# Adding the last three token tiles of expert 0 from PSUM instead of from memory, and routing tiles 5 to 8 one step sooner

## The chip, the cores and the metric

The kernel runs on one core of a Trainium2 chip, as one program. The metric is device time in microseconds (us) of one execution. Within the core TensorE (PE) multiplies, VectorE (DVE), ScalarE (ACT) and GpSimd (POOL) do the rest of the arithmetic, and SyncE (SP) issues most transfers; each engine works through its own queue in order and waits for the others by semaphores.

## The reference, cut to what matters

```python
x = attention(q, k, v, proj)                       # 1536 tokens x 512
h = x @ w_in; e = exp(h - max(h)); solu = h * e / (sum(e) + 1e-9)
x = (layernorm(solu) * g_ln) @ w_out               # 1536 x 512, hidden 1024
logits = x @ w_gate                                # 8 experts
e_idx = argmax(logits); gate_w = softmax(logits)[e_idx]
eom = 1 / (1 + exp(-(x @ w_output_gate)))
for e in range(8):
    m = e_idx == e
    out[m] = gate_w[m] * eom[m, e] * (relu(x[m] @ w1[e]) @ w2[e])
```

## The kernel before, in words

The program has three stages on PE: attention (to about 210 us), the dense block (class Ffn) on twelve tiles of 128 tokens (to about 370 us), and the eight experts (class Experts) to the end. Products are made of float32 split into a high and a low part (hi, lo), three products for one.

In the dense block each tile i goes through `up` (two halves of 512), `solu` (DVE and ACT), `turn` (PE transposes), `down` (24 products into `y` or `h`, copied by ACT to `row`), `flip` (PE transposes of the row), and `logits` or `batch` (products with the gate weights). Tiles are routed in GROUPS: 0 to 4, 5 to 8, 9 and 10, and 11. `route(g)` returns two lists: `first` finds the expert of each token (DVE), and `rest` counts, by small PE products (`ranks`), which place the token has among those of its expert, works out a `slot`, and then POOL writes (`scatter`) the 515-column rows (512 values, gate, token number, expert) to those slots of a buffer in memory, `scratch`, by one indirect transfer for each tile. Each expert has CAP = 256 slots. Lists of `route` wait in `stages` until `flush` runs them, or until they are merged with `solu`; PE, DVE, ACT and POOL each run their share in the order in which the program was written.

In the stage of the experts `rows(e)` reads the 256 rows of an expert back from `scratch` (two transfers on SP), `turn(e)` transposes them on PE and splits them into `xh` and `xl` (ACT and DVE), `up(e)` and `down(e)` make the two layers, and `finish` scales and writes to the output. `fetch(u)` loads a unit of weights (1 MB) and `splitw(u)` makes its high and low part, mostly an expert ahead. `early` splits units 0 and 1 during the end of the dense block.

The two stages meet so: the rows of expert 0 are read when all twelve scatters have landed (`rows`, line 1033, with a wait for each scatter), and until they come PE does 28 products that nobody reads (`warm`, line 1068). SP's queue holds, in this order, the reads of experts 0, 1 and 2 (six transfers) and then the loads of the weight units from 4 on.

Of the kernel before, what the change touches and what calls it, by code (L numbers as in the profile page):

```python
# [8 lines left out]
F32 = mybir.dt.float32  # L9
F32R = mybir.dt.float32r  # L10
# [562 lines left out]

def merge(a, b):
    k = -(-len(b) // max(1, len(a)))
    for f in a:
        f()
        for g in b[:k]:
            g()
        b = b[k:]  # L580
    for g in b:
        g()


class Ffn:
# [3 lines left out]
    def __init__(self, tc, ctx, C, xT, W, scratch, cnt):  # L589
        self.tc, self.nc, self.C, self.xT = tc, tc.nc, C, xT  # L590
# [4 lines left out]
        self.ep = pool("ep", 2)  # L595
# [10 lines left out]
        self.wo = W.wo  # L606

# [87 lines left out]
    def down(self, i, mid=None, wide=False):  # L695
# [10 lines left out]
        st["row"] = self.grp[g][:, i - a, 0:DM]  # L706
# [68 lines left out]
    def scatter(self, row, slot):  # L775
# [3 lines left out]
        apart(self.tc, "rows", ins, self.C["gap"])  # L779
        self.sent.append(ins)  # L780

    def route(self, g):
# [32 lines left out]
        ]  # L815
        if n == 1:
# [70 lines left out]
    def run(self, ahead, blank):  # L887
# [26 lines left out]
        for t in range(n):  # L914
# [29 lines left out]
            if t == n - 1:  # L944
# [3 lines left out]
                merge(ops[3:], pend)  # L948
# [5 lines left out]
            if t == 0:  # L954
                self.split(3)
                blank(self.gp.tile([P, DM], F32, name="zero"))
                continue
# [7 lines left out]
        self.down(n - 2, {8: lambda: self.flip(n - 3, True)}, True)  # L965
        flush()
# [12 lines left out]
        early(4)  # L979


class Experts:
    def __init__(self, tc, C, stg, w1, w2, scratch, out):
        self.tc, self.nc, self.C = tc, tc.nc, C
# [8 lines left out]
    def open(self, ctx):  # L993
# [3 lines left out]
        self.hp = pool("he", 2)  # L997
# [29 lines left out]

    def rows(self, e):
        nc = self.nc
        st = self.st[e] = {"r": [], "id": []}  # L1030
        for t in range(2):
            r = self.rp.tile([P, ROW], F32, tag=f"r{t}", name=f"r{t}")
            ins = nc.sync.dma_start(out=r, in_=self.scratch[e * CAP + t * P:e * CAP + t * P + P, :])
            for x in self.sent if e == 0 and t == 0 else ():
                info = mybir.DependencyInfo(mybir.DependencyClass.Sync, mybir.DependencyReason.DATA)
# [281 lines left out]
```

## Time and profile before

| what | us |
|---|---|
| median of 3 runs | 576.09 (575.34 to 576.25) |
| the profiled execution | 575.28 |
| its span, first to last instruction | 573.5 |

The profiled execution has 1.78 us outside its span. Times in the rows below are microseconds from the start of the span unless marked ns; a row of the timeline merges neighbouring instructions of a kind (x8), and an engine's own clock position is what ties rows of different engines together.

### The profile page before, as it was taken

Reading aid. Unit: us, or ns where it says so; the run is one execution under the profiler, and the core shown is the slowest. Engines: PE = TensorE matmul, PEld = TensorE weight load, DVE = VectorE, ACT = ScalarE, POOL = GpSimd, SP = SyncE. Lnnn points to the kernel's source line nnn. Section 1 sums busy time; section 2 is a strip of 40 time slices with the busy share of each in tenths; the row PEclk is TensorE's granted clock in tenths of the full one; section 3 lists DMA queues with packets and bytes.
Section 4 is the critical chain, followed back from the end, with each engine's and each line's share of the span. In section 5 each row is a group of like instructions: output and inputs, shape, how many; then the busy total and the mean of one; then the engine's idle time right before and its main releaser. Section 6 shows DMA issues by size and latency. Waiting matters only on the chain. (4 is left out here: it accounts for less than half of the span.)

```text
span 573.5 us, 9895 instructions
## 1 busy us (share of the span) xinstructions
PE 558.1 (97%) x3830; PEld 443.5 (77%) x3830; DVE 392.4 (68%) x788; ACT 266.1 (46%) x450; POOL 331.1 (58%) x269
## 2 busy tenths in 40 slices
PE   8899999999999999999999999899999999999996
PEld 3666677766677557888888888788989989899894
DVE  7978788898888666877688665736564563655631
ACT  3556757576576533223333222517255453463530
POOL 5499889898989862100000310517695865957741
PEclk9999999999999999999999999999999999999998
DMA  3545636555453465200000130284649458387200
GB/s 110 172 129 157 174 114 195 140 148 152 142 134 120 95 210 197 108 0 1 2 0 1 56 38 1 110 270 154 209 172 327 141 219 279 128 319 248 75 23 36
DMA packets 47812, 76.08 MB, mean 133 GB/s; under 512 B 11275, under 2 KB 20235, under 8 KB 47758
## 3 DMA queue, kind: packets, MB, share of 16 engines
q1 hardware_dynamic: 42622, 59.49, 32.6%
q10 hardware_dynamic: 2896, 9.57, 5.4%
q0 software_dynamic: 2240, 6.31, 3.3%
q8 instruction: 32, 0.52, 0.4%
q14 instruction: 22, 0.18, 0.1%
HBM read 58.39 MB, written 17.93 MB: 133 GB/s over the span
## 5 line engine op out<-in xcount | busy, mean ns | idle before, releaser
L1024 POOL TENSOR_TENSOR wl<-ws,wh 128x512 fp32r<-128x512 f32 x75 | 107.2, 1462 | 53.5 <-ACT wh L1022 53.5
L283 POOL TENSOR_TENSOR acc<-pt,pt 128x768 f32<-128x768 f32 x48 | 90.0, 1877 | 28.8 <-ACT pt L279 27.0
L255 DVE TENSOR_REDUCE m<-ps 128x2 f32<-128x768 f32 x96 | 87.8, 949 | 11.2 <-PE ps L243 8.6
L279 ACT ACTIVATE pt<-ps 128x768 f32<-128x768 f32 x96 | 76.5, 814 | 37.1 <-PE ps L243 37.0
L1022 ACT CAST wh<-ws 128x512 fp32r<-128x512 f32 x128 | 70.4, 618 | 5.1 <-POOL wl L1024 2.6
L294 PE MATMUL ps<-pt,v 128*64 128x385 f32 x384 | 67.1, 493 | 0.0
L609 POOL TENSOR_TENSOR xl<-xT,xh 128x512 fp32r<-128x512 f32 x12 | 15.6, 1305 | 86.0 <-ACT xh L618 56.1
L1024 DVE TENSOR_TENSOR wl<-ws,wh 128x512 fp32r<-128x512 f32 x53 | 57.3, 1115 | 10.7 <-ACT wh L1022 9.0
L1090 DVE SCALAR_TENSOR_TENSOR hl<-g,hh 128x512 fp32r<-128x512 f32 x32 | 22.1, 691 | 59.9 <-ACT hh L1089 49.3
L1089 ACT ACTIVATE hh<-g 128x512 fp32r<-128x512 f32 x32 | 19.1, 598 | 81.4 <-PE g L1084 58.0
L285 POOL TENSOR_TENSOR acc<-acc 128x768 f32<-128x768 f32 x30 | 54.9, 1829 | 2.4
L294 PEld LDWEIGHTS ps<-pt,v 128*64 128x64 f32 x384 | 25.6, 136 | 34.3 <-issue 30.4
L1106 PE MATMUL o<-wh,hh 128*128 128x512 f32 x128 | 51.1, 399 | 0.0
L1106 PE MATMUL o<-wl,hh 128*128 128x512 f32 x128 | 50.5, 394 | 0.0
L1106 PE MATMUL o<-wh,hl 128*128 128x512 f32 x128 | 50.5, 394 | 0.0
L627 PE MATMUL h<-wi,xh 128*128 128x512 f32 x192 | 49.4, 399 | 0.0
L627 PE MATMUL y<-wo,lh 128*128 128x512 f32 x176 | 42.6, 394 | 0.0
L1084 PE MATMUL g<-xh,wh 128*128 128x256 f32 x256 | 41.2, 283 | 0.3 <-ACT xh L1053 0.3
L1084 PE MATMUL g<-xl,wh 128*128 128x256 f32 x256 | 41.2, 282 | 0.0
L1084 PE MATMUL g<-xh,wl 128*128 128x256 f32 x256 | 40.9, 282 | 0.0
L627 PEld LDWEIGHTS h<-wi,xh 128*128 128x128 f32 x192 | 34.9, 188 | 7.4 <-ACT xh L618 0.6
L776 POOL DMA_INDIRECT scratch<-row,slot x12 | 12.6, 1048 | 47.3 <-DVE cnt L801 29.9
(217 smaller groups left out, 1179.5 us busy)
## 6 DMA issues: line engine op xcount, KB each, us to landing
ws<-in_moe_w_dram SPq DMA_DIRECT2D x32, 1024.0 KB
scratch<-zero SPq DMA_DIRECT2D x7, 1030.0 KB
r<-scratch SPq DMA_DIRECT2D x16, 257.5 KB
raw<-in_moe_w_in_dram ACTq DMA_DIRECT2D x8, 512.0 KB
raw<-in_moe_w_out_dram ACTq DMA_DIRECT2D x8, 512.0 KB
v<-in_v_dram SPq DMA_DIRECT2D x8, 384.0 KB
out_dram<-zero SPq DMA_DIRECT2D x3, 1024.0 KB
q<-in_q_dram SPq DMA_DIRECT2D x7, 384.0 KB
```

The source lines that it names most:

```text
L255: nc.vector.tensor_reduce(out=st["m", i][:, c, :, kh], in_=ps, axis=AX.X, op=ALU.max, negate=True)
L279: nc.scalar.activation(out=pt[:, :, 0:HW], in_=ps, func=AF.Exp, scale=0.125)
L283: nc.gpsimd.tensor_tensor(out=acc, in0=st["pt", i, c - 1][:, :, 0:HW], in1=pt[:, :, 0:HW], op=ALU.add)
L285: nc.gpsimd.tensor_tensor(out=acc, in0=parts.pop(), in1=acc, op=ALU.add)
L294: nc.tensor.matmul(st["x", i][D * h:D * h + D, 0:HW + 1], st["v"][:, h, c, :], st["pt", i, c][:, h, 0:HW + 1], start=(c == 0), stop=(c == ...
L627: nc.tensor.matmul(ps, a[:, k, :], w[j](k), start=(n == 0), stop=(n == len(jobs) - 1))
L1022: nc.scalar.copy(hi[:, k, :], t[:, k, :])
L1024: eng.tensor_tensor(out=lo[:, k, :], in0=t[:, k, :], in1=hi[:, k, :].bitcast(F32), op=ALU.subtract)
L1084: nc.tensor.matmul(ps[:, a, :], w[:, k, f * P:(f + 1) * P], x[:, k, :], start=(n == 0), stop=(n == 11))
L1089: nc.scalar.activation(out=hi, in_=ps, func=AF.Relu)
L1090: nc.vector.scalar_tensor_tensor(out=hl[:, 2 * g:2 * g + 2, :], in0=ps, scalar=0.0, in1=hi.bitcast(F32), op0=ALU.max, op1=ALU.subtract)
L1106: nc.tensor.matmul(st["o"][t], h[:, f, t * P:(t + 1) * P], w[:, f % 4, :], start=(f == 0 and n == 0), stop=(f == 7 and n == 2),)
```

## The change

The rows of expert 0 are no longer read when all scatters have landed. `Experts.first` reads them (both transfers, full rows) as soon as the scatters of tiles 0 to 8 have, and the scatters of tiles 9 to 11 wait until that read is done; slots that those tiles will fill hold zeros then. `collect` transposes what was read into two PSUM tiles without ending their accumulation, and `place(i, n)` adds the rows of tile i to half n of them by two float32 products with a matrix of 0 and 1 (128 tokens x 256 slots), which `spots` in `route` makes on DVE by comparing an `iota` of 0 to 255 with the slot of each token. `take` splits the sum into `xh` and `xl`. `Experts.rest` reads the three last columns of the rows (gate, token number, expert) again when all scatters have landed; `ids` uses them after the second step of expert 0.

`first` of the group of tiles 5 to 8 is merged with `solu` of tile 11, and `rest` stands in `down` of tile 10 (after 4 of 24 products) instead of after it. For tiles 9 and 10 `logits` and `first` move from after 16 to after 8 products of `down` of tile 11, and `rest` from after it to after 18 products. `warm` is gone. The tiles `hh` and `hl` of the experts now lie where `w_out` was.

```diff
-    def scatter(self, row, slot):
+    def scatter(self, row, slot, late):
         ins = self.nc.gpsimd.indirect_dma_start(
             out=self.scratch, out_offset=bass.IndirectOffsetOnAxis(ap=slot, axis=0), in_=row, in_offset=None
         )
         apart(self.tc, "rows", ins, self.C["gap"])
+        for x in self.ex.read if late else ():
+            depend(self.tc, ins, x, "rows were read before")
         self.sent.append(ins)
...
+        def spots(x, y):
+            f = t("sf", [P, n, 1])
+            ops = [lambda: tt(f, x, y, ALU.add)]
+            for i in range(n):
+                self.spot[a + i] = t(f"oh0{i}", [P, CAP])
+                ops.append(lambda i=i: ts(self.spot[a + i], self.iota, f[:, i], None, ALU.is_equal, ALU.bypass))
+            return ops
...
+                *spots(s1.unsqueeze(1), b1.unsqueeze(1)),
                 lambda: tt(slot[:, 0, :], s1, b1, ALU.add),
...
                 lambda: tt(slot, s1, s2, ALU.add),
+                *(spots(s1, s2) if g > 1 else ()),
             ]
-        rest += [lambda i=i: self.scatter(row[:, i, :], slot[:, i, 0:1]) for i in range(n)]
+        rest += [lambda i=i: self.scatter(row[:, i, :], slot[:, i, 0:1], g > 1) for i in range(n)]
...
-                merge(ops[3:], pend)
+                merge(ops[3:], stages.pop(0))
...
-        self.down(n - 2, {8: lambda: self.flip(n - 3, True)}, True)
-        flush()
+        def mid():
+            flush()
+            self.ex.first(self.sent)
+
+        self.down(n - 2, {4: mid, 8: lambda: self.flip(n - 3, True)}, True)
         self.logits(n - 3)
         self.turn(n - 1)
         self.flip(n - 2, True)
-        flush()
         early(4)
-        self.down(n - 1, {16: lambda: (gate(n - 2), flush())})
-        flush()
+        self.down(n - 1, {8: lambda: (gate(n - 2), flush()), 18: flush})
+        self.collect()
         self.flip2(n - 1)
+        self.place(n - 3, 0)
         gate(n - 1)
         flush()
+        self.place(n - 3, 1)
+        self.place(n - 2, 0)
         flush()
+        self.place(n - 2, 1)
+        for k in range(2):
+            self.place(n - 1, k)
+        self.ex.rest(self.sent)
+        self.ex.take([self.ep.tile([P, FF], F32, tag="e", name="e") for _ in range(2)], self.x0)
...
+    def collect(self):
+        self.x0 = []
+        for n in range(2):
+            ps = self.pt.tile([P, 4, P], F32, tag="t", name="t").rearrange("p (a b) n -> p a (b n)", a=2)
+            for k in range(2):
+                for t, r in enumerate(self.ex.st[0]["r"]):
+                    x = r[:, (2 * n + k) * P:(2 * n + k + 1) * P]
+                    self.nc.tensor.matmul(
+                        ps[:, k, t * P:(t + 1) * P], x, self.C["ident"], start=(k + t == 0), stop=False, is_transpose=True
+                    )
+            self.x0.append(ps)
+
+    def place(self, i, n):
+        row = self.st_row[i]
+        for k in range(2):
+            x = row[:, (2 * n + k) * P:(2 * n + k + 1) * P]
+            self.nc.tensor.matmul(self.x0[n][:, k, :], x, self.spot[i], start=False, stop=(k == 1 and i == 2 * NC - 1))
...
+    def first(self, sent):
+        st = self.st[0] = {"r": [], "id": []}
+        self.read = []
+        for t in range(2):
+            r = self.rp.tile([P, ROW], F32, name=f"r0{t}")
+            ins = self.nc.sync.dma_start(out=r, in_=self.scratch[t * P:t * P + P, :])
+            for x in sent if t == 0 else ():
+                depend(self.tc, ins, x, "rows come from every scatter so far")
+            self.read.append(ins)
+            st["r"].append(r)
+
+    def rest(self, sent):
+        for t, r in enumerate(self.st[0]["r"]):
+            ins = self.nc.sync.dma_start(out=r[:, DM:ROW], in_=self.scratch[t * P:t * P + P, DM:ROW])
+            for x in sent if t == 0 else ():
+                depend(self.tc, ins, x, "rows come from every scatter")
...
-        for e in range(2):
-            self.rows(e)
-        self.warm(28)
-        self.turn(0)
+        self.st[0]["id"] = [self.sp.tile([P, 1], I32, tag="id", name="id") for _ in range(2)]
+        self.rows(1)
...
+                if (e, s) == (0, 1):
+                    self.ids(0)
```

On PE, between the end of `down` of tile 11 and the first product of expert 0 (`h` and `lg` are PSUM tiles of `flip2`, of the logits and of the ranks; L732 is the transposition of tile 11's row, L743 its logits, L766 to L773 its ranks), this stood before:

```order
L732 MATMUL h<-ident,row_4294 128x128 x4
L743 MATMUL lg<-wg_76,yT 128x16 x4
L766 MATMUL lg<-cnt,ident 128x8
L769 LDWEIGHTS tri
L769 MATMUL lg<-oh_4354,tri 128x8
L773 LDWEIGHTS onesb
L773 MATMUL lg<-oh_4354,onesb 128x8
L1068 MATMUL g<-wh 128x512 x28
```

And this stands there now (`t` are the two PSUM tiles of `collect`, whose eight transposes, L1020, stand just ahead of these rows; `oh_4281`, `oh_4282` and `oh_4384` are the 0/1 matrices of tiles 9, 10 and 11; the numbers of the lines have moved by 7):

```order
L739 MATMUL h<-ident,row_4337 128x128 x4
L1029 MATMUL t<-oh_4281,row_4134 128x256 x2
L750 MATMUL lg<-wg_76,yT 128x16 x4
L1029 MATMUL t<-oh_4281,row_4134 128x256 x2
L1029 MATMUL t<-oh_4282,row_4134 128x256 x2
L773 MATMUL lg<-cnt,ident 128x8
L776 LDWEIGHTS tri
L776 MATMUL lg<-oh_4381,tri 128x8
L780 LDWEIGHTS onesb
L780 MATMUL lg<-oh_4381,onesb 128x8
L1029 MATMUL t<-oh_4282,row_4134 128x256 x2
L1029 MATMUL t<-oh_4384,row_4337 128x256 x4
```

The 28 products of `warm` are gone; the twelve products L1029 of `place` are new, two of them ahead of tile 11's logits, four between these and tile 11's ranks, and six behind the ranks; the first product of expert 0 follows.

On SP, behind the last transfer that clears the output, this stood before (L1033 are the reads of the rows, L1011 the weights):

```order
L1236 DMA out_dram<-zero 512x1x512 x3
L1033 DMA r_4421<-scratch 128x515
L1033 DMA r_4424<-scratch 128x515
L1033 DMA r_4427<-scratch 128x515
L1033 DMA r_4430<-scratch 128x515
L1033 DMA r_4480<-scratch 128x515
L1033 DMA r_4483<-scratch 128x515
L1011 DMA ws<-in_moe_w_dram 128x4x512 x4
```

And now (L1082 is `first`, L1090 `rest`, L1118 `rows` of experts 1 and 2, L1060 the weights):

```order
L1315 DMA out_dram<-zero 512x1x512 x3
L1082 DMA r_4182<-scratch 128x515
L1082 DMA r_4184<-scratch 128x515
L1090 DMA r_4182<-scratch 128x3
L1090 DMA r_4184<-scratch 128x3
L1118 DMA r_4468<-scratch 128x515
L1118 DMA r_4471<-scratch 128x515
L1118 DMA r_4474<-scratch 128x515
L1118 DMA r_4477<-scratch 128x515
L1060 DMA ws<-in_moe_w_dram 128x4x512 x4
```

The two reads of expert 0 stand where they stood, with a wait for nine scatters in place of twelve; two small reads, which wait for all twelve, stand between them and the reads of experts 1 and 2.

On DVE, behind the small operations of tiles 9 and 10 (`s` and `slot` are the slot's parts and the slot), this stands now:

```order
L810 TENSOR_TENSOR slot_4279<-s_4275,s_4276 128x2
L810 TENSOR_TENSOR sf_4280<-s_4275,s_4276 128x2
L811 TENSOR_SCALAR oh_4281<-iota,sf_4280 128x256
L811 TENSOR_SCALAR oh_4282<-iota,sf_4280 128x256
L810 TENSOR_TENSOR cnt<-cnt,lg 128x8
L740 COPY yT<-h 128x256
L813 TENSOR_REDUCE m_4371<-lg 128x1
```

The rows `sf` and `oh` are new there (three of them for these two tiles; for tile 11 the like two stand just ahead of its slot).

## Rows read from the trace of the kernel before

**Rows 1.** PE timeline from tile 9's logits to expert 0 (start, length, what, idle before).

```profile
356.73 1.04 PE L743 MATMUL lg<-wg,yT 128*128 128x16 f32 x8 [0.41 <-DVE lz L851]
...
365.80 0.20 PE L769 MATMUL lg<-oh,tri 128*128 128x8 bf16 x2
...
366.42 0.71 PE L732 MATMUL h<-ident,row 128*128 128x128 f32 x4 [0.34 <-ACT row L708]
...
367.65 1.03 PE L743 MATMUL lg<-wg,yT 128*128 128x16 f32 x8 [0.52 <-DVE cnt L801]
...
370.00 0.39 PE L766 MATMUL lg<-cnt,ident 128*128 128x8 f32 x2 [1.31 <-DVE s L802]
...
370.29 8.21 PE L1068 MATMUL g<-wh 128*128 128x512 f32 x28
...
378.96 0.98 PE L1051 MATMUL x<-ident,r 128*128 128x128 f32 x7 [0.36 <-DMA r<-scratch]
...
380.24 1.00 PE L1084 MATMUL g<-xh,wh 128*128 128x256 f32 x4 [0.29 <-ACT xh L1053]
```

**Rows 2.** DVE timeline of the same stretch.

```profile
351.79 1.00 DVE L677 TENSOR_SCALAR e<-e,mv,s 128x512 f32<-128x512 f32 x2
...
360.17 0.16 DVE L802 TENSOR_SCALAR ix<-cm 128x4 f32<-128x4 f32 x1
...
361.72 0.16 DVE L801 TENSOR_TENSOR slot<-s,s 128x4 int32<-128x4 f32 x1
...
370.47 0.17 DVE L803 SCALAR_TENSOR_TENSOR rk<-lg,oh 128x8 f32<-128x8 f32 x1
...
371.13 0.16 DVE L801 TENSOR_TENSOR slot<-s,b 128x1 int32<-128x1 f32 x1
...
379.99 0.69 DVE L1053 CAST xh<-x 128x512 fp32r<-128x512 f32 x1 [4.18 <-PE x L1051]
```

**Rows 3.** POOL timeline: scatters of tiles 0, 4, 5 and 11.

```profile
324.62 1.21 POOL L776 DMA_INDIRECT scratch<-row,slot  x1 [14.16 <-DVE mv L661]
...
329.92 0.96 POOL L776 DMA_INDIRECT scratch<-row,slot  x1 [0.19 <-issue]
...
362.16 1.25 POOL L776 DMA_INDIRECT scratch<-row,slot  x1 [29.91 <-DVE cnt L801]
...
372.12 0.96 POOL L776 DMA_INDIRECT scratch<-row,slot  x1 [1.59 <-ACT wh L1022]
```

**Rows 4.** SP's queue after the last scatter (timeline).

```profile
375.52 2.76 SPq L1033 DMA_DIRECT2D r<-scratch  x6
...
378.38 16.99 SPq L1011 DMA_DIRECT2D ws<-in_moe_w_dram  x4
```

**Rows 5.** SP's waits ahead of line 1033 (count, ns min/median/max, first and last start).

```profile
L1033 SPq EVENT_SEMAPHORE  x11: 17/28/39765, 335.5 to 405.3; - x11
```

**Rows 6.** PE timeline: float32 products of 384 columns in attention.

```profile
208.13 1.46 PE L314 MATMUL ps<-acc,ones 128*64 128x384 f32 x8
```

**Rows 7.** The same line in the list by line and shape (busy us, mean ns).

```profile
L314 PE MATMUL ps<-acc,ones 128*64 128x384 f32 x72 | 14.6, 489 | 0.2 <-POOL acc L283 0.2
```

**Rows 8.** PE timeline: products of 256 columns in expert 0, split float32.

```profile
383.20 0.64 PE L1084 MATMUL g<-xl,wh 128*128 128x256 f32 x4
...
383.68 0.64 PE L1084 MATMUL g<-xh,wh 128*128 128x256 f32 x4
```

**Rows 9.** Windows: length, busy time of each engine, granted clock, DMA share, GB/s.

```profile
366.00:370.00 4.00, 1.83 (x17) 1.37 (x13) 2.64 (x22) 1.11 (x4) 3.29 (x7) 1.00 0.52 202
...
371.00:372.00 1.00, 1.00 (x5) 0.82 (x5) 0.42 (x5) 1.00 (x4) 0.00 (x0) 0.85 0.65 251
...
372.00:375.00 3.00, 3.00 (x8) 2.32 (x8) 1.77 (x4) 0.59 (x2) 1.08 (x2) 0.50 0.26 93
...
375.00:376.00 1.00, 1.00 (x5) 0.81 (x5) 0.80 (x2) 0.00 (x0) 0.00 (x0) 0.94 0.00 0
...
400.00:420.00 20.00, 20.00 (x136) 18.43 (x134) 11.17 (x16) 9.47 (x18) 14.36 (x14) 1.00 0.68 235
```

More of the change, by code (lines that the diff above doesn't have):

```diff
@@ L571, in apart, with depend @@
     tc.add_to_no_dep_group(group, ins)
+def depend(tc, ins, on, why):
+    info = mybir.DependencyInfo(mybir.DependencyClass.Sync, mybir.DependencyReason.DATA)
+    tc.add_manual_dep(ins.ins, on.ins.name, info, reason=why)
 def merge(a, b):
@@ L606, in __init__ @@
         self.wo = W.wo
+        self.iota = self.gp.tile([P, CAP], F32, name="iota")
+        self.spot, self.st_row = {}, {}
     def sub(self, eng, out, x, hi):
@@ L956, in run @@
                 blank(self.gp.tile([P, DM], F32, name="zero"))
+                nc.gpsimd.iota(
+                    self.iota, pattern=[[1, CAP]], base=0, channel_multiplier=0, allow_small_or_imprecise_dtypes=True
+                )
                 continue
@@ L1026, in splitw, with take, ids @@
         return [lambda k=k: part(k) for k in range(4)]
+    def first(self, sent):
[13 more added lines that the diff above has]
+                depend(self.tc, ins, x, "rows come from every scatter")
+    def take(self, e, half):
+        nc, st = self.nc, self.st[0]
+        xh, xl = (t.rearrange("p (k n) -> p k n", k=4).bitcast(F32R) for t in e)
+        st["xh"], st["xl"] = xh, xl
+        for n, ps in enumerate(half):
+            (nc.scalar.copy if n == 0 else nc.vector.tensor_copy)(xh[:, 2 * n:2 * n + 2], ps)
+        for n, ps in enumerate(half):
+            w = slice(2 * n, 2 * n + 2)
+            nc.vector.scalar_tensor_tensor(
+                out=xl[:, w], in0=xh[:, w].bitcast(F32), scalar=-1.0, in1=ps, op0=ALU.mult, op1=ALU.add
+            )
+    def ids(self, e):
+        st = self.st[e]
+        for t in range(2):
+            self.nc.vector.tensor_scalar(
+                out=st["id"][t], in0=st["r"][t][:, DM + 1:DM + 2], scalar1=float(OFF), scalar2=None, op0=ALU.add
+            )
     def rows(self, e):
@@ L1032, in rows @@
             r = self.rp.tile([P, ROW], F32, tag=f"r{t}", name=f"r{t}")
-            ins = nc.sync.dma_start(out=r, in_=self.scratch[e * CAP + t * P:e * CAP + t * P + P, :])
-            for x in self.sent if e == 0 and t == 0 else ():
-                info = mybir.DependencyInfo(mybir.DependencyClass.Sync, mybir.DependencyReason.DATA)
-                self.tc.add_manual_dep(ins.ins, x.ins.name, info, reason="rows come from every scatter")
+            nc.sync.dma_start(out=r, in_=self.scratch[e * CAP + t * P:e * CAP + t * P + P, :])
             st["r"].append(r)
@@ L1058, in turn @@
             )
-        for t in range(2):
-            nc.vector.tensor_scalar(
-                out=st["id"][t], in0=st["r"][t][:, DM + 1:DM + 2], scalar1=float(OFF), scalar2=None, op0=ALU.add
-            )
+        self.ids(e)
     def warm(self, n):
@@ L1071, in up @@
         nc, st = self.nc, self.st[e]
-        hh = st["hh"] = self.hp.tile([P, 8, CAP], F32R, tag="hh", name="hh")
-        hl = st["hl"] = self.hp.tile([P, 8, CAP], F32R, tag="hl", name="hl")
+        b = 4 * (e % 2)
+        hh, hl = st["hh"], st["hl"] = [t[:, b:b + 4, :].rearrange("p k (a n) -> p (k a) n", a=2) for t in self.hs]
         xh, xl = st["xh"], st["xl"]
@@ L1264, in tile_kernel @@
         stg = c4.enter_context(tc.tile_pool(name="ws", bufs=4, reuse_waits="tile"))
-        ex = Experts(tc, C, stg, moe2_w1, moe2_w2, scratch, out)
+        ep = c4.enter_context(tc.tile_pool(name="ep", bufs=2, reuse_waits="tile"))
+        r0 = c4.enter_context(tc.tile_pool(name="r0", bufs=1, reuse_waits="tile"))
+        ex = Experts(tc, C, stg, moe2_w1, moe2_w2, scratch, out, r0, W.wo)
         with ExitStack() as c2:
-            ffn = Ffn(tc, c2, C, xT, W, scratch, cnt)
+            ffn = Ffn(tc, c2, C, xT, W, scratch, cnt, ep, ex)
             for u in range(4):
```

15 lines of the change are left out of this document (7 added, 8 removed).

## The prediction

> **What bounds the kernel now.** I read the profile in this order: the timeline of PE around the change, those of DVE, POOL and SP on the same clock, then the granted clock by windows. Once the experts run, PE is the bound: it is busy for all of the 20.00 us from 400 to 420 [rows 9]. What PE loses ahead of them is therefore lost to the whole kernel, and what it gains there is kept, if nothing behind takes it back. The seam between the dense block and the experts is such a loss. Tile 11's last rank products are over at about 370.3, and the first product of expert 0 starts at 380.24 [rows 1]. The 8.21 us of products between them [rows 1] are filler: PE looks busy and makes nothing. What ends the wait is a chain over three engines: DVE has tile 11's slot at 371.13 [rows 2], POOL issues its scatter at 372.12 [rows 3], SP can issue the reads only at 375.52 [rows 4], the second half of the rows is there at 378.96 [rows 1], and the copies of the transposed rows start on DVE at 379.99 [rows 2]. From slot to copy that is 8.86 us.
>
> **What the change does to that chain.** It takes memory out of it. Behind tile 11's ranks there now stand on DVE the slot's number and its 0/1 matrix, then four products of `place` on PE, then the copies. I need three prices.
>
> The 0/1 matrix is a tensor_scalar of 256 columns. Two of 512 columns took 1.00 us [rows 2], so it costs between 0.25 (half of one) and 0.5; I take 0.3, since most of such an operation goes with its columns.
>
> A float32 product of 256 columns is not in the trace. Such products are two instructions each there (four products of the logits are x8 [rows 1]). On the line of attention's sums, where two products for the two heads run side by side, eight instructions are four steps: 1.46 us, less 0.489 for the last alone [rows 6, 7], is 0.97 for three, or 0.32 a step of 384 columns. For 256 columns that gives 0.216, and two of them 0.43 a product. The lower bound is split products of 256 columns, four in 383.68 - 383.20 = 0.48 [rows 8], so twice 0.12 or 0.24. The upper bound is 0.86, all of it at half the clock. I take 0.43, from the same kind of operand.
>
> On the path behind tile 11's slot: its number takes the place of the slot at 371.13, the matrix starts 0.2 later and takes 0.3, PE follows in 0.1, four products take 1.72, their result needs about 0.2 to be seen, and the copy starts at 373.65 by the old clock instead of 379.99. That is 6.3 us less.
>
> **What it adds ahead of it.** Tile 11's ranks come later, because PE does other things first. `down` of tile 11 ends at 365.80 as before: for it the two groups' rank products, a few tenths, have moved inside, and the idle 0.41 in front of tile 9's logits goes [rows 1], since the transposition that DVE was asked for there now stands before `down` of tile 9. Behind it come the eight transposes of `collect` (seven took 0.98 [rows 1], so 1.0), the four of `flip2` (0.5, their idle 0.34 covered by `collect`) and one `place` (two products, 0.86), and tile 11's logits start at 368.15, against 367.65 [rows 1]. The wait of 0.52 that they had [rows 1] is used. Between logits and ranks PE idled 1.31 [rows 1]; there now stand two `place`, 1.72, and the ranks start at about 370.75 against 370.00, 0.75 later. The last `place` of tile 10 (0.86) lies beside DVE's 0.66 from ranks to slot (370.47 to 371.13 [rows 2]) and the matrix, and costs nothing; without that cover it would cost 0.86.
>
> Sum: 6.3 - 0.75, or 5.6 us less. The profiled execution goes from 575.28 to 569.7 (span 573.5 to 567.9); the median of the runs stands 0.8 above it, at 576.09, and so goes to **570.5**. The low price of the products would take about another 1.5 off (a shorter `place` before the logits 0.4, the ranks then bound by DVE 0.4, tile 11's four products 0.75): 569.0.
>
> **Edits at no cost, and what hides them.** The `iota` is one operation on POOL where it waits for products anyway. Tiles 5 to 8's `first` is six small operations among `solu` of tile 11; operations of this kind run 0.08 apart (360.17 to 361.72 for 20 [rows 2]), so `solu` ends about 0.5 later than 352.79 (351.79 + 1.00 [rows 2]), more than 3 us before PE wants it. Unit 1 of the weights is now split behind the copies and not in the filler's time: four operations on ACT and on DVE, some 2.5 us, wanted by expert 0's third group of products about 6 us after its start; without that slack PE would wait up to 2.5. SP's later queue (two small reads, four reads, then unit 4) starts with tile 11's scatter, about 0.75 later than before, while expert 0 starts 5.6 sooner: the loads, from 378.38 before [rows 4], lose 6.4 us against PE. Unit 4 is first wanted by the products of expert 1, over 20 us behind, and the reads of expert 1 by its transposition, some 20 us behind too; the list of waits names no transfer as a releaser of any engine after expert 0's start, so this is covered. The three columns that `rest` reads are wanted by DVE after expert 0's second group and block little behind them.
>
> **The early read** must be there when `collect` comes, at 365.8. Tile 5's slots: `solu` over at 353.3, then the operations that took from 360.17 to 361.88 [rows 2], so 355.0; POOL starts 0.28 later, as it did at 362.16 [rows 3], 355.3; the fourth scatter is issued three spacings of 1.33 on (five issues from 324.62 to 329.92 [rows 3]), 359.3; from the last issue to SP's read were 3.40 (372.12 to 375.52 [rows 3, 4]), 362.7; from there to the second half of the rows 3.44 [rows 1, 4], with six reads then in the queue and two now: 366.1 at the latest. So it comes within some tenths of PE's arrival, and I count no wait, with 0.3 as the upper bound on this reckoning. There is no slack beyond that, and behind the waiting transposes stand tile 11's transposition, logits and ranks, and with them everything.
>
> **Rivals.**
>
> Late read. Tile 4's scatter, the last of five in a row, was issued at 329.92 [rows 3], and the first wait recorded behind SP's wait for it starts at 335.5 [rows 5]: 5.6 us, not 3.40. If the four scatters of tiles 5 to 8 are like that, the rows come at 368.3 and PE waits 2.5: **573.0**. For it speaks that they too are issued one behind another; against it that scatters from 362 on, spaced nearly as closely, were quick. 0.15.
>
> The clock falls. From 366 to 370 PE was busy for 1.83 of 4.00 us, and behind it the granted clock fell: 0.85, 0.50 and 0.94 in the windows from 371 to 376 [rows 9], the lower of the two levels (1.2 of 2.4 GHz) for about 3.4 us, all of it under the filler. Now there is no filler, and a fall would lie over useful products: 3.4 us at half speed lose 1.7, so **572.2**. Against it: in the same 4 us PE now does 1.0 + 0.5 + 0.86 + 1.0 and part of the next 1.72, with almost no gap. For it: transposes and logits are narrow products, and every wait of the late read's kind adds a gap. The Trainium skill ("TensorE: Matmul & The Clock Gate", What's actually happening) says "the default state is throttled, and activity releases the throttle"; by that rule taking the filler away costs speed where expert 0 starts, and the trace agrees that the clock fell behind the half-idle stretch. 0.17. With the late read together, 574.7: 0.05.
>
> The gain is given back: expert 1's weights, 6.4 us later against PE, hold up ACT's splits and by them PE. Then the loads are the bound and the end stays: **576**. Against it stands the list of waits. 0.04.
>
> Slower: the read of expert 0 is in front of tile 11 in PE's queue, so each microsecond that it is late costs one. With the copies in hand 5.6 us earlier, it decides against the change once the rows come more than 5.6 us after PE, later than 371.4; that takes scatters that land one behind another, each as slowly as tile 4's (four times 5.6 behind 355.3 is 377.7, and the rows at 381.1). PE would then wait about 15 us, **585**. Nothing in the trace shows scatters that don't overlap. A milder form ends at about 578. 0.04.
>
> **How the numbers follow.** My forecast has 0.55, between 569.0 and 571.4 (the low price of the products; a read some tenths late, a dearer matrix). Faster by over 0.2% (1.15 us, about what a measurement of this kernel can tell from no change) are it, the late read, the fall of the clock and most of their joint case: 0.88. Within 0.2% are the gain given back and the rest of the joint case: 0.07. Slower 0.05. The range from 568.8 to 574.4 takes in the low price and both single rivals.
>
> **What would show it.** Right: the first product of expert 0 at about 374.3 in the span's time, the four last `place` just ahead of it and back to back at 0.43 each; the first read issued by SP at 362 to 363; `collect` with an idle of a few tenths at most; tile 11's ranks at 370 to 371; the granted clock at 1.00 through the seam; as much PE time behind expert 0's start as before. Wrong: an idle of microseconds ahead of `collect`, released by the read; windows at 0.50 between 366 and 380; ACT's splits in expert 0 waiting for a transfer; PE idle in expert 0 for unit 1's low part.

## The result, and the profile after

The changed kernel takes 565.51 us (median of 4 runs, 564.93 to 566.14) against 575.72 us (574.84 to 576.25) for the kernel before on the same chip: 10.2 us less, a ratio of 0.982 (0.981 to 0.984). The direction was right, but the forecast of 570.5 us and its range (568.8 to 574.4) were not. The profiled execution took 566.14 us, 9.1 less than the one of the kernel before (575.28); its span is 564.4 us.

PE's timeline of the changed kernel at the seam, which answers to [rows 1]:

```profile
365.70 1.64 PE L634 MATMUL y<-wo,ll 128*128 128x512 f32 x6
367.18 1.19 PE L1020 MATMUL t<-ident,r 128*128 128x128 f32 x8
368.21 0.60 PE L739 MATMUL h<-ident,row 128*128 128x128 f32 x4
368.65 1.03 PE L1029 MATMUL t<-oh,row 128*128 128x256 f32 x4
369.51 0.96 PE L750 MATMUL lg<-wg,yT 128*128 128x16 f32 x8
370.32 1.97 PE L1029 MATMUL t<-oh,row 128*128 128x256 f32 x8
372.13 0.28 PE L773 MATMUL lg<-cnt,ident 128*128 128x8 f32 x2
...
372.32 1.11 PE L1029 MATMUL t<-oh,row 128*128 128x256 f32 x4
373.76 1.99 PE L1029 MATMUL t<-oh,row 128*128 128x256 f32 x8 [0.33 <-DVE oh L811]
375.57 0.50 PE L1163 MATMUL g<-e,wh 128*128 128x256 f32 x2
376.54 0.50 PE L1163 MATMUL g<-e,wh 128*128 128x256 f32 x2 [0.47 <-DVE e L1099]
```

The transposes of the early read follow `down` of tile 11 with no idle time: the read came in time. The first `place` (two products, four instructions) takes 0.86 from its start to the next start (368.65 to 369.51), 0.43 a product. Behind tile 11's ranks there is no memory any more; the filler (8.21 us in [rows 1]) is gone. DVE's timeline of the same stretch, which answers to [rows 2]:

```profile
373.16 0.16 DVE L810 TENSOR_TENSOR sf<-s,b 128x1 f32<-128x1 f32 x1
373.35 0.35 DVE L811 TENSOR_SCALAR oh<-iota,sf 128x256 f32<-128x256 f32 x1
373.62 0.15 DVE L810 TENSOR_TENSOR slot<-s,b 128x1 int32<-128x1 f32 x1
...
375.79 0.69 DVE L1099 CAST e<-t 128x512 fp32r<-128x512 f32 x1 [1.89 <-PE t L1029]
```

And the windows of the changed kernel (length, busy time of each engine, granted clock, DMA share, GB/s), against the fall to 0.50 in [rows 9]:

```profile
366.00:370.00 4.00, 4.00 (x28) 3.40 (x26) 2.33 (x18) 1.15 (x4) 1.60 (x3) 1.00 0.27 98
370.00:372.00 2.00, 2.00 (x13) 1.82 (x13) 1.32 (x11) 0.42 (x3) 0.55 (x2) 1.00 0.54 208
372.00:374.00 2.00, 1.67 (x11) 1.19 (x10) 1.37 (x12) 0.06 (x1) 0.00 (x0) 1.00 0.00 0
374.00:376.00 2.00, 2.00 (x10) 1.49 (x9) 0.21 (x1) 1.07 (x3) 1.07 (x2) 1.00 0.03 8
376.00:378.00 2.00, 1.53 (x11) 1.28 (x11) 2.00 (x5) 1.59 (x4) 0.00 (x0) 1.00 0.37 140
...
380.00:400.00 20.00, 20.00 (x127) 17.87 (x126) 13.69 (x20) 13.02 (x25) 15.96 (x12) 1.00 0.99 340
```

The surprise stands behind the seam. From expert 0's first product to the end of the span were 573.5 - 380.24 = 193.26 us; now they are 564.4 - 375.57 = 188.83, 4.43 less, though no product was taken away there. The transpositions for experts 1 and 7 bound six whole experts. In the kernel before:

```profile
399.19 1.03 PE L1051 MATMUL x<-ident,r 128*128 128x128 f32 x8
...
540.00 1.04 PE L1051 MATMUL x<-ident,r 128*128 128x128 f32 x8
```

In the changed one:

```profile
394.98 1.03 PE L1133 MATMUL x<-ident,r 128*128 128x128 f32 x8
...
531.64 1.03 PE L1133 MATMUL x<-ident,r 128*128 128x128 f32 x8
```

That is 23.47 us an expert before and 22.78 after. PE is never idle in either, and the granted clock is 1.00 in both, so the products themselves must follow each other faster. Groups of four 256-column products start 0.48 apart in [rows 8]; in the changed kernel's expert 1 the timeline has them 0.45 to 0.46 apart, about 114 ns each instead of about 119:

```profile
404.08 0.62 PE L1163 MATMUL g<-xh,wh 128*128 128x256 f32 x4
404.54 0.62 PE L1163 MATMUL g<-xh,wl 128*128 128x256 f32 x4
404.99 0.62 PE L1163 MATMUL g<-xl,wh 128*128 128x256 f32 x4
```

In the dense block it goes the other way. The groups by line and shape from 220 to 350 us (busy us, mean ns of one), before:

```profile
L627 PE MATMUL h<-wi,xh 128*128 128x512 f32 x165 | 42.6, 400 | 0.0
L627 PE MATMUL y<-wo,lh 128*128 128x512 f32 x160 | 38.7, 394 | 0.0
```

and after:

```profile
L634 PE MATMUL h<-wi,xh 128*128 128x512 f32 x166 | 42.9, 400 | 0.0
L634 PE MATMUL y<-wo,lh 128*128 128x512 f32 x160 | 39.4, 397 | 0.0
```

The second dense product became dearer by 3 ns in its duration, and by 5 in the distance of its starts (228.1 to 233.3 ns, means over 230 to 350 us), with the same instructions.

### The profile page after: what moved, and what is told of

Its sections match the earlier page's. It is cut to its first block, busy times and chain, and to the rows that moved or that the text cites. A ratio compares the mean times of both kernels' runs of the same rounds, so it can differ in the third digit from the quotient of the medians.

```text
span 564.4 us, 9890 instructions
## 1 busy us (share of the span) xinstructions
PE 551.3 (98%) x3826; PEld 438.2 (78%) x3826; DVE 393.2 (70%) x793; ACT 266.1 (47%) x450; POOL 330.3 (59%) x270
## 5 line engine op out<-in xcount | busy, mean ns | idle before, releaser
L1185 PE MATMUL o<-wh,wo 128*128 128x512 f32 x256 | 82.6, 394 | 0.0
L1169 DVE SCALAR_TENSOR_TENSOR wo<-g,wo 128x512 fp32r<-128x512 f32 x32 | 22.1, 691 | 53.2 <-ACT wo L1168 53.2
L1185 PEld LDWEIGHTS o<-wh,wo 128*128 128x128 f32 x256 | 48.1, 188 | 9.7
L1168 ACT ACTIVATE wo<-g 128x512 fp32r<-128x512 f32 x32 | 19.1, 598 | 75.7 <-PE g L1163 75.7
L1185 PE MATMUL o<-wl,wo 128*128 128x512 f32 x128 | 50.2, 392 | 0.0
L634 PEld LDWEIGHTS y<-wo,lh 128*128 128x128 f32 x176 | 32.4, 188 | 7.8 <-issue 0.2
L243 PE MATMUL ps<-Hk,Hq 64*128 64x384 f32 x192 | 36.9, 375 | 1.1 <-DVE m L255 0.7
L243 PE MATMUL ps<-Hq,Hk 64*128 64x384 f32 x192 | 35.2, 363 | 1.0 <-DVE m L255 1.0
```

What stands on the lines that cost most here:

```text
L243: self.nc.tensor.matmul(ps[:, h], w[r], x[r], start=(n == 0), stop=(n == len(jobs) - 1), tile_position=(D * h, 0))
L634: nc.tensor.matmul(ps, a[:, k, :], w[j](k), start=(n == 0), stop=(n == len(jobs) - 1))
L1168: nc.scalar.activation(out=hi, in_=ps, func=AF.Relu)
L1169: nc.vector.scalar_tensor_tensor(out=hl[:, 2 * g:2 * g + 2, :], in0=ps, scalar=0.0, in1=hi.bitcast(F32), op0=ALU.max, op1=ALU.subtract)
L1185: nc.tensor.matmul(st["o"][t], h[:, f, t * P:(t + 1) * P], w[:, f % 4, :], start=(f == 0 and n == 0), stop=(f == 7 and n == 2),)
```

## What differs: the places of the tiles

The change opens two pools earlier, drops the hidden layer's pool and puts hh and hl into w_out's tiles. So most tiles start at another byte of the partition. Theory A: the distance of products depends on where the moving and the stationary tile start. Theory B: the seam's history, or other traffic, makes the experts faster. These are the starts that the allocation gives, modulo 256, and the difference d = moving - stationary modulo 256:

```
product (columns)        moving, stationary     before              changed
dense first (512)        wi,    xh              224-160: d 64       224-224: d 0
dense second (512)       wo,    lh and ll       160-160: d 0        160-224: d 192
experts' first (256)     xh xl, wh and wl        96-224: d 128      160-224: d 192
experts' second (512)    wh wl, hh and hl       224- 96: d 128      224-160: d 64
```

## Experiments

**Only the place of the experts' xh and xl.** In the kernel before (the hidden layer's pool is then moved on by 960 more):

```diff
+        gap = lambda n, b: pool(n, 1).tile([P, b // 4], F32, name=n)
+        gap("g0", 64)
         self.xp = pool("xe", 2)
```

> The kernel before, with 64 unused bytes per partition ahead of the tiles of the experts' turned rows (xh and xl), so that they start 672 instead of 608 bytes past a multiple of 1024, as they do in the changed kernel; the tiles of the hidden layer are moved by a whole 1024. No instruction is changed. Theory A (where an operand of a product lies in SBUF sets how far apart products start): the 256-column products of experts 1 to 7 start every 113 ns instead of 119, the 512-column ones every 232 as before; 8 experts with 96 products each by 6 ns are 4.6 us, so about 571.2 us (570.5 to 572.5). Theory B (the changed kernel's experts run faster because of what goes on in the seam ahead of them, or because of other traffic): 119 ns and 575.7 us as before.

Measured: 571.62 us, ratio 0.9945 (0.9928 to 0.9961). Theory B falls: 64 unused bytes bring 3.6 us. The groups from 400 to 530 us (busy us, mean ns of one), the kernel before and then this one:

```profile
L1084 PE MATMUL g<-xh,wh 128*128 128x256 f32 x184 | 29.4, 282 | 0.0
```

```profile
L1087 PE MATMUL g<-xh,wh 128*128 128x256 f32 x192 | 29.8, 277 | 0.0
```

The mean duration of a product fell from 282 to 277 ns. It came 1.0 us short of 4.6: the mean distance fell from 119.0 to about 113.5 and not by 6 ns (8 x 96 x 5.4 = 4.15), and expert 4 ran at 118 ns, 0.4 us more; a later run shows that products at these places have two distances.

**The same 64 bytes in the changed kernel.** The same pad ahead of its "xe" pool (d 0).

> The changed kernel, with 64 unused bytes per partition ahead of the tiles of the experts' turned rows, so that they start 736 instead of 672 bytes past a multiple of 1024 (96 instead of 32 past a multiple of 128, as in the kernel before). No instruction is changed. Theory A: 256-column products of experts 1 to 7 go back to one every 119 ns; 7 by 96 by 6 ns are 4.0 us, so about 569.5 us (568.3 to 570.3). Theory B: 113 ns and 565.5 us, as in the changed kernel.

Measured: 569.24 us (565.51 without it), ratio to before 0.9899 (0.9883 to 0.9916). From 400 to 530 us, the changed kernel and then this one:

```profile
L1163 PE MATMUL g<-xh,wh 128*128 128x256 f32 x192 | 29.7, 277 | 0.0
```

```profile
L1165 PE MATMUL g<-xh,wh 128*128 128x256 f32 x188 | 30.1, 282 | 0.0
```

So 3.7 us of the changed kernel's gain hang on one pool's start.

**Only the hidden layer in w_out's tiles**, in the kernel before:

```diff
-        self.hp = pool("he", 2)
...
-        hh = st["hh"] = self.hp.tile([P, 8, CAP], F32R, tag="hh", name="hh")
-        hl = st["hl"] = self.hp.tile([P, 8, CAP], F32R, tag="hl", name="hl")
+        b = 4 * (e % 2)
+        hh, hl = st["hh"], st["hl"] = [t[:, b:b + 4, :].rearrange("p k (a n) -> p (k a) n", a=2) for t in self.hs]
```

> The kernel before, with the hidden layer of the experts (hh, hl) written into the space of w_out's two tiles as in the changed kernel; nothing else is changed, and no other tile moves. Theory A: the 512-column products of the experts start every 227 to 230 ns instead of 232, so 8 by 48 by 2 to 5 ns are 0.8 to 1.9 us less; 256-column products stay at 119 ns: 573.8 to 574.9 us. Theory C (the whole gain of the experts' stage, up too, comes from where the hidden layer lies or from its pool's waits): 113 ns and about 571.2 us. Theory B: 575.7 us.

Measured: 574.60 us, ratio 0.9985 (0.9976 to 0.9995). The 512-column products stand 229.3 ns apart instead of 232.4, the 256-column ones 119.6. By the first 1.2 us were due; 0.6 came, part of it taken back by the second. Theory C falls.

**Only the dense tiles**, in the changed kernel:

```diff
+        pool("g0", 1).tile([P, 16], F32, name="g0")
         self.xp = pool("xp", 2)
```

> The changed kernel, with 64 unused bytes per partition ahead of the dense block's tiles (xh, xl, lh, ll), so that they start 32 instead of 96 bytes past a multiple of 128, as in the kernel before; the experts' tiles stay. No instruction is changed. Theory A: the 512-column products of the dense block on lh and ll start every 227 ns instead of 233; 11 tiles behind the first by 24 products by 6 ns are up to 1.6 us, and about 1.2 us by the distance of the tiles in the two traces: about 564.3 us (563.7 to 565.0), the experts at 113 ns as in the changed kernel. Theory B: 565.5 us.

Measured: 566.49 us, 1.0 more and not 1.2 less. The rule on which I had put it (the start modulo 128) was wrong: the second dense products stood 232.6 ns apart (d 128), and the first went from 229.7 to 233.0 (d 192).

**Places alone.** TensorE with nothing beside it.

> Leaves the whole computation out: TensorE alone, 128 groups of products in the kernel's form (a new stationary 128x128 for each, moving rows of 256 columns, 24 products in a group, or of 512 columns, 16 products), one group for each pair of starts of the stationary and the moving tile, at 0, 32, ... 224 bytes past a multiple of 256; then all groups again in the opposite order. No other engine and no DMA works meanwhile. Theory A (place alone): the distance of two starts depends on the pair of places, with about 113 and about 119 ns at 256 columns, and 227 and 233 ns at 512, and is the same in both orders. Theory D (the place matters only by a clash with what other engines or transfers read and write): all pairs at one distance, near 107 to 113 ns and 213 to 227 ns.

Mean distance in ns by the start of the stationary tile (rows, modulo 256) and of the moving one (columns), first order, every second row, in one execution; the granted clock is 1.00 throughout:

```
256 columns     0     32     64     96    128    160    192    224
  0         119.7  118.0  118.0  119.6  118.7  117.4  113.7  118.0
 64         117.8  118.3  119.7  118.0  118.0  119.6  118.7  117.4
128         118.4  117.3  114.8  118.0  119.7  118.0  118.0  119.6
192         117.8  119.8  118.8  117.4  117.7  118.2  119.7  118.0
512 columns     0     32     64     96    128    160    192    224
  0         227.3  233.5  229.7  233.2  232.9  234.3  232.8  232.8
 64         233.1  232.9  228.3  233.5  229.7  233.2  232.9  234.3
128         232.3  234.1  233.7  232.9  228.3  233.5  229.7  233.2
192         228.8  233.2  232.9  234.3  232.7  232.8  227.1  233.5
```

Each row is the one above, moved two columns on: at 512 columns only the difference d counts, with 227 to 229 ns at d 0, 229 to 230 at 64 and 232 to 235 elsewhere, and both orders agree to 2 ns. At 256 columns nearly all is at about 117 to 120, but d 192 has two distances: in the first order 113.7 to 114.8 for five of the eight starts and 117.7 to 117.8 for three, in the opposite one 117.7 to 118.0 for all. (One group of d 64 stood at 113.5 in that order.) In the trace's own rows (count: shortest, median and longest duration in ns, first and last start) the groups of d 0, 128 and 192 at 256 columns and of d 0 and 128 at 512:

```profile
L35 PE MATMUL ps<-B,A x24: 278/283/283, 32.1 to 34.9; 128*128 128x256 f32 x24
...
L39 PE MATMUL ps<-B,A x24: 279/281/285, 43.5 to 46.3; 128*128 128x256 f32 x24
...
L41 PE MATMUL ps<-B,A x24: 276/276/279, 49.2 to 51.8; 128*128 128x256 f32 x24
...
L99 PE MATMUL ps<-B,A x16: 388/389/395, 213.6 to 217.0; 128*128 128x512 f32 x16
...
L103 PE MATMUL ps<-B,A x16: 390/395/398, 228.4 to 231.9; 128*128 128x512 f32 x16
```

Theory D falls: no other engine is needed. The Trainium skill ("SBUF — State Buffer", SBUF: two separate sides) says that PE's port waits on no other engine; this run agrees as far as it goes, since the spread is all there with TensorE alone.

**The places without the change.** The kernel before, every tile where the changed kernel has it (its pools opened in that order), its own instructions.

> The kernel before, its instructions unchanged in kind, order and number (but for the two unused tiles), with every tile of the dense block and of the experts at the place that it has in the changed kernel, and the hidden layer in w_out's tiles. Theory A: the places give the 4.4 to 4.6 us of the experts and cost the 1.2 us of the dense block: 575.5 - 4.5 + 1.2 = about 572.2 us (571.2 to 572.8); the seam's own gain is then 572.2 - 565.5 = 6.7 us, between 5.7 and 7.3. If instead the seam's own sum of the forecast (5.6 us) holds to a few tenths, 571.1 us. Theory B (the seam brings the whole gain): 575.5 us.

Measured: 572.07 us, ratio 0.9938 (0.9920 to 0.9955). So the places alone are worth 575.42 - 572.07 = 3.35 us, and the change of the program 572.07 - 565.51 = 6.6. In the profiled execution the experts take 5.3 less than before and the dense block 1.3 more, but the old seam is also 1.0 longer: 15.29 us from the end of `down` of tile 11 to expert 0's first product, where it is 14.29 in the kernel before and 13.93 to 14.83 in the other runs here that keep the whole old program.

**And the routing sooner, without the early read** (in the same places; only the edits of the routing are shown):

```diff
-                merge(ops[3:], pend)
+                merge(ops[3:], stages.pop(0))
...
-        self.down(n - 2, {8: lambda: self.flip(n - 3, True)}, True)
-        flush()
+        self.down(n - 2, {4: flush, 8: lambda: self.flip(n - 3, True)}, True)
...
-        flush()
         early(4)
-        self.down(n - 1, {16: lambda: (gate(n - 2), flush())})
-        flush()
+        self.down(n - 1, {8: lambda: (gate(n - 2), flush()), 18: flush})
```

> The kernel before in the changed kernel's places, and with the routing of tiles 5 to 8 and of tiles 9 and 10 at the points where the changed kernel has it; expert 0's rows are still read after every scatter and turned by TensorE, so the early read and the products with 0/1 matrices are left out. By the forecast these edits cost and bring nothing: the time of the kernel before in these places to 0.5 us (about 572). Rival: the earlier ranks of tile 11 (its slot within the chain) bring up to 1 us themselves: about 571.

Measured: 570.77 us, ratio 0.9915 (0.9899 to 0.9932): 1.3 us less than without (570.66 to 570.91 against 571.22 to 572.78), where the forecast had nothing. PE's and DVE's timelines, first with the old routing, then with the new:

```profile
357.86 1.04 PE L743 MATMUL lg<-wg,yT 128*128 128x16 f32 x8 [0.41 <-DVE lz L851]
...
368.81 1.04 PE L743 MATMUL lg<-wg,yT 128*128 128x16 f32 x8 [0.47 <-DVE slot L801]
...
370.82 0.17 DVE L804 TENSOR_REDUCE m<-lg 128x1 f32<-128x8 f32 x1 [1.82 <-PE lg L743]
```

```profile
357.56 0.96 PE L743 MATMUL lg<-wg,yT 128*128 128x16 f32 x8
...
368.13 1.06 PE L743 MATMUL lg<-wg,yT 128*128 128x16 f32 x8 [0.24 <-ACT yT L733]
...
369.23 0.17 DVE L804 TENSOR_REDUCE m<-lg 128x1 f32<-128x8 f32 x1 [0.88 <-PE lg L743]
```

The idle 0.41 is gone, and tile 11's logits start 0.68 sooner. Another 0.93 stands between them and DVE: with the old routing DVE read them 0.97 us after PE's last modelled end (369.85), with the new 0.04. The kernel before has 0.30 there (368.68 to 368.98), and the last run below, with the same instructions, 0.03. Why it was late here was not found. Expert 0's first product comes 1.78 sooner (382.46 to 380.68), but from there to the end 0.6 is given back (187.90 to 188.51): with the same starts, expert 0's 256-column products stand 117.6 apart instead of 113.5, and the first 30 of its 512-column ones 233 instead of 229.

**How long the pattern is.**

> Leaves the whole computation out: TensorE alone, as in the run before, with the stationary tile fixed and the moving tile's start moved in steps of 32 bytes through 1024 (48 products of 256 columns a group, in three orders; 24 of 512 columns, in two orders) and by 4 to 28 bytes from a few starts. If only the difference of the two starts modulo 256 matters: the same distance at d, d+256, d+512 and d+768; 512 columns near 228 ns at 0, 230 at 64, 232 to 234 elsewhere; 256 columns near 113 or 118 ns at 192, 120 at 0, 117 to 120 elsewhere. If a longer period matters, the four quarters differ.

All four quarters agree: 512 columns stand at a median of 227 ns at 0, 256, 512 and 768, 229 to 230 at 64, 320, 576 and 832, and mostly 231 to 237 elsewhere. 256 columns stand at 120 at d 0. At d 192 every group took one of two distances: 118 in the rising order, all four times; 113 or 118 in the others. Behind its first few products a group stayed in its state. Some starts that are no multiple of 32 bytes apart were dearer (121 to 124 ns at 4, 20, 68 and 196).

**The changed kernel with d 0 wherever 512 columns move:**

```diff
+        c4.enter_context(tc.tile_pool(name="g0", bufs=1)).tile([P, 16], F32, name="g0")
         keep = c4.enter_context(tc.tile_pool(name="wo", bufs=1))
...
+        c4.enter_context(tc.tile_pool(name="g1", bufs=1)).tile([P, 48], F32, name="g1")
         ep = c4.enter_context(tc.tile_pool(name="ep", bufs=2, reuse_waits="tile"))
```

> The changed kernel, with 64 unused bytes ahead of w_out's tiles and 192 ahead of the pool of the erf's tiles, so that the difference of starts (moving minus stationary, modulo 256) is 0 for both dense products and for the experts' 512-column products (192 and 64 in the changed kernel), and 192 for the experts' 256-column products (as in the changed kernel). No instruction is changed. If the difference modulo 256 sets the distance: the dense second product at 227 to 228 ns instead of 233 (about 1.4 us in all), the experts' 512-column products at 227 to 228 instead of 230 (8 by 48 by 2.5 ns, about 0.9 us), so about 563.2 us (562.3 to 564.5). Rival (start modulo 128 alone): no gain, 565.5 us.

Measured: 565.83 us, not 563.2. All 512-column products did go to 227 ns (229 in the dense first), but the experts' 256-column ones fell into the other state of d 192: 118 ns in experts 1 to 7. That costs 7 x 96 x 4.2 = 2.8 us and eats the rest.

**The kernel before with d 0 in the same way** (pads ahead of the dense xh, lh, the experts' xh, and hh).

> The kernel before, with 64 unused bytes ahead of the dense xh and xl, 192 ahead of lh, 64 ahead of the experts' xh and xl and 64 ahead of the hidden layer, so that the difference of starts modulo 256 is 0 for the dense products (64 and 0 before) and for the experts' 512-column products (128 before), and 192 for the experts' 256-column products (128 before). No instruction is changed. If the difference sets the distance: 256-column products at 113 instead of 119 ns (4.6 us), 512-column ones of the experts at 228 instead of 232 (1.5 us), the dense first products at 228 instead of 230 (0.5 us): about 568.8 us (568.0 to 570.0), and the changed kernel in its best places 5.5 to 6.7 us below it.

Measured: 572.27 us, not 568.8, ratio 0.9948 (0.9932 to 0.9965), and again 113 ns in expert 0 and 118 behind it. In both kernels, d 0 in the experts' second product goes with 118 in the next expert's first; with d 64 or 128 it was 113, but for one expert.

**So only the dense tiles are mended:**

```diff
+        pool("g0", 1).tile([P, 48], F32, name="g0")
         self.lp = pool("lp", 2)
```

> The changed kernel, with 192 unused bytes ahead of the dense lh and ll alone, so that both dense products stand at a difference of starts of 0 modulo 256 (0 and 192 in the changed kernel); the experts keep 192 at 256 columns and 64 at 512. No instruction is changed. The dense second product at 227 instead of 233 ns gives back about 1.4 us of the dense block (12 tiles by 24 products by 5 to 6 ns are 1.4 to 1.7, of which the first tiles overlap); if the experts' 256-column products stay in the shorter of their two distances (113 ns), 564.1 us (563.5 to 564.8), the fastest yet. If they fall into the longer one (118 ns), about 567 us.

Measured: 564.21 us, ratio 0.9803 (0.9788 to 0.9818), the lowest of all kernels here, though its interval overlaps that of the changed kernel. Its groups in the dense block and in the experts have the shorter products of both kinds:

```profile
L635 PE MATMUL y<-wo,lh 128*128 128x512 f32 x160 | 38.6, 393 | 0.0
...
L1164 PE MATMUL g<-xh,wh 128*128 128x256 f32 x188 | 29.1, 277 | 0.0
```

In the profiles its dense block is 1.3 us shorter than the changed kernel's, the seam 0.5 longer, and the stretch from expert 0's first product on 0.5 shorter; this last was luck, since expert 0, with unchanged starts, took 113.5 instead of 117.8.

**And the kernel before in like places** (d 0, 0, 192 and 64; the pads of `e8` in the table below, the kernel before with d 0, without the last).

> The kernel before, with the same differences of starts as in the run above for all four kinds of products (64 unused bytes ahead of the dense xh and xl, 192 ahead of lh, 64 ahead of the experts' xh and xl). No instruction is changed. 256-column products of the experts at 113 instead of 119 ns (4.6 us), their 512-column ones at 230 instead of 232 (0.8 us), the dense first product at 228 to 231 as before or slightly less (0 to 0.5): about 569.6 us (568.8 to 570.7). The changed kernel in the same places is then 5 to 6.7 us faster, which is what the seam alone is worth; the forecast gave it 5.6.

Measured: 570.00 us, ratio 0.9902 (0.9886 to 0.9917). With the same distances of all products, the seam alone is worth 570.00 - 564.21 = 5.8 us; the forecast gave it 5.6. Some of the 5.8 is this run's own filler:

```profile
370.75 9.34 PE L1073 MATMUL g<-wh 128*128 128x512 f32 x28
379.92 1.03 PE L1056 MATMUL x<-ident,r 128*128 128x128 f32 x8
```

It took 9.34 us against 8.21 [rows 1], with the clock granted at 0.50 from 370 to 376, and the transposes follow it without a wait for the rows. By estimate, the rows would have allowed the first product at 380.74 (376.02, SP's read here, and 3.44 and 1.28 as before [rows 1, 4]) instead of 381.25: 0.5 us.

The mean distances in ns of neighbouring products, from which these follow (steps over a gap left out; dense from 230 to 350 us, experts 1 to 7 from 400 to 560):

```
kernel                    dense 1st  dense 2nd  exp.0 1st  exp. 1st  exp. 2nd   us
before                      229.5      228.1      118.6     119.0     232.4    575.7
changed                     229.7      233.3      117.8     113.6     228.9    565.5
e4 changed, dense +64       233.0      232.6      117.6     113.6     228.9    566.5
e5 before, its places       229.7      233.3      113.5     113.6     228.9    572.1
e6 e5, routed sooner        229.8      233.3      117.6     113.5     229.0    570.8
e7 changed, d 0             228.9      227.2      113.5     117.8     227.0    565.8
e9 changed, dense d 0       230.3      227.6      113.5     113.5     228.9    564.2
e8 before, d 0              230.3      227.6      113.9     117.8     226.9    572.3
e10 before, like e9         230.2      227.6      113.7     113.6     228.9    570.0
```

From before to changed that is 7 x 96 x 5.4 = 3.6 and 7 x 48 x 3.5 = 1.2 us in experts 1 to 7 and 0.1 in expert 0 (less the 0.47 that expert 0 waits for its copies: the 4.4 above), and 12 x 24 x 5.2 = 1.5 lost in the dense block. From the end of attention to the end of `down` of tile 11 the profiles have 155.26 us before, 156.53 with the changed kernel's places, 156.24 with the sooner routing too and 156.21 in the changed kernel.

One column follows d only in part: the dense first products go to 233.0 at d 192 (e4), but at d 0 (the changed kernel and all rows below it but e4) they stand at 228.9 to 230.3, no nearer than at d 64 before (229.5). Why d 0 gains nothing there, no run shows.

## Why the prediction was wrong

**The sum over the seam was right.** From the end of `down` of tile 11 to DVE's copy were 14.03 us (365.96 to 379.99), now 8.45 (367.34 to 375.79): 5.58 less, forecast 6.3 - 0.75 = 5.6. Its terms:
- The 0/1 matrix took 0.35 (0.3), `place` 0.43 a product (0.43), and from the slot's number to the copy it was 2.63 us (373.16 to 375.79; forecast 2.52).
- Tile 11's ranks start 4.79 behind the end of `down` against 4.04: 0.75 later, as forecast.
- The read was in time, so that rival did not come. It is as tight as it looked: where `down` of tile 11 ends 1.37 sooner (365.97, the changed kernel with its dense tiles moved) `collect` waits 0.26 for it, within the 0.3 of the bound.
- The clock stayed at 1.00 from 366 to 380. That rival fell because `collect` and `place` fill what was idle: PE is busy for 4.00 of 4.00 us from 366 to 370, against 1.83 in [rows 9]. In e5, e6 and e10 of the table, which have the old seam, it was busy for 3.04, 2.49 and 2.29, and the clock fell to 0.50 behind. The rule of the Trainium skill cited with that rival ("TensorE: Matmul & The Clock Gate", What's actually happening) agrees with both sides.
- Loads come later and nobody waits for them: but for the 0.47 ahead of its second pair of products, expert 0 keeps PE busy (20.00 of 20.00 us from 380 to 400), unit 1's late split included. The gain was not given back.

**What failed is a step that was taken for granted: "as much PE time behind expert 0's start as before", and `down` of tile 11 ending "at 365.80 as before".** Neither holds: the experts took 4.43 us less, and `down` ended 1.38 later (367.34 against 365.96). Of the 1.38, 0.44 stood already at the end of attention (210.69 and 211.13), which no edit touches and which lies anywhere from 210.25 to 211.33 in these kernels; 0.95 came in the dense block. The experts' gain and the dense block's loss come from the tiles' places, which the sum left out though the change moves the pools: 3.35 us net with the old program. That is most of the 4.6 by which the forecast missed. In the two profiled executions the sum closes: 6.05 in the seam, counted to expert 0's first product (14.28 to 8.23), and 4.43 behind it, less 1.38, are the 9.1 by which the spans differ. With `down` the signs on the span's clock came late: SP's first read at 364.00 and not 362 to 363, tile 11's ranks at 372.13 and not 370 to 371, expert 0 at 375.57 and not 374.3.

**One edit costed at nothing did not come out as nothing:** the sooner routing brought 1.3 us in these places. What it is worth elsewhere is open. The dense block is 0.3 shorter with it (156.53 to 156.24), where the forecast set the idle 0.41 ahead of tile 9's logits against the rank products moved into `down`. The seam is 1.3 shorter (15.29 to 13.97), but against the 14.29 of the kernel before it would be 0.3; so about 1.0 seems to belong to that one run's long seam. The early read and the sum in PSUM alone are worth 570.77 - 565.51 = 5.3 us: these two kernels have the same places and the same routing, and expert 0 at the same distances.

**The range** was built from costs and waits of the changed instructions alone. But for the fall of the clock, no rival had unchanged instructions running at another speed.

## What to carry to other kernels

A change that opens, drops or reorders pools moves every tile behind them, and with them the speed of products that nobody edited; compare the distance of starts of unchanged products first, before explaining a difference by the edit. To weigh a change of program alone, give the kernel before the same places. Where a kernel is bound by TensorE, a few unused bytes ahead of a pool are worth trying, but over the whole chain of products: the best place for one kind may put the next into its slower state.

## What the runs showed of the hardware

- The distance of products whose stationary tile changes each time depends on (start of the moving tile - start of the stationary tile) modulo 256 bytes: at 512 columns of split float32 227 to 229 ns at 0, 229 to 230 at 64, about 232 to 235 at the other multiples of 32; at 256 columns about 117 to 120, and 113 or 118 at 192. TensorE alone shows it, at a granted clock of 1.00. In the kernels the experts' products and the dense second ones follow it, the dense first ones only in part (233 ns at 192, but 229 to 230 at 0). Why the start matters, no run shows.
- At d 192 there are two steady states, and what ran before seems to decide between them; which predecessor gives which was not settled (in the experts a 512-column product with d 0 ahead went with 118 ns, one with d 64 or 128 with 113 but for one expert; by themselves, two groups of 256 columns with d 64 went ahead of 118). Expert 0 of the changed kernel shows two states at d 64 and 512 columns as well: about 233 ns for its first 30 products and, behind a gap of 1 us, 229.
- The Trainium skill ("TensorE: Matmul & The Clock Gate", Back-to-back issue gap) gives 262 and 518 cycles for a single product of 256 and 512 columns by itself, by estimate 109 and 216 ns at 2.4 GHz. No place reached that here: 113 and 227 ns were the least.
